# Another fixed order for layer 1, with sixteen more unread products, ten of them in a second bank, and ten instead of thirteen ahead of it

## The chip, the cores and the metric

One core of a Trainium2 chip runs the whole program. The core has five engines that each work through their own instructions in order: TensorE (PE, matmuls; its weight loads are listed as PEld), VectorE (DVE), ScalarE (ACT), GpSimd (POOL) and SyncE (SP), which here only starts DMA transfers. The metric is the device time of one execution in microseconds (us); lower is better.

## The reference

Three stages follow one another: an mLSTM, a gated layer and a normed gated layer.

```python
for t in range(S):                       # q, k, v: (2, 8, 768, 40)
    m_new = np.maximum(f_gate[:, :, t] + m, i_gate[:, :, t])
    f_stab = np.exp(f_gate[:, :, t] + m - m_new)
    i_stab = np.exp(i_gate[:, :, t] - m_new)
    C = f_stab[..., None, None] * C + i_stab[..., None, None] * np.einsum('bhd,bhe->bhde', vt, kt)
    n = f_stab[..., None] * n + i_stab[..., None] * kt
    y[:, :, t] = sigmoid(o_gate[:, :, t]) * (C @ qt) / np.maximum(np.abs(n . qt), 1.0)
x = y.transpose(0, 2, 1, 3).reshape(1536, 320)
x = (sigmoid(x @ w_gate) * (x @ w_val)) @ w_out            # layer 1: 320 -> 1536 -> 320
xn = x / np.sqrt(np.mean(x * x, -1, keepdims=True) + 1e-06) * rms_g
g = xn @ w_gate2
out = (g * sigmoid(g) * (xn @ w_val2)) @ w_out2            # layer 2: the same sizes
```

## The kernel before

The mLSTM is computed in six chunks c of 128 steps for each of the two batches b. A chunk needs scores (`S`, PE line 335), decays by a scan (`F`, DVE line 237), their product (`P`, DVE line 234), the part inside the chunk (`PV`, PE line 427), the part from the state (`I`, PE line 402) and a state update (`U`). Layers 1 and 2 run over twelve blocks f of 128 hidden columns. For layer 1, the operation `Tcf` (PE line 577, sixteen matmuls) multiplies chunk c by block f; for chunks 4 and 5 together it is `Tpf0` and `Tpf1` (PE line 623, eight matmuls of 512 columns each). `Y` operations multiply the hidden values by the block's output weights. Layer 2 starts inside the same fixed order with blocks 0 to 4 of its first four row tiles (`Tq`, `Yq`), and the rest of it is a loop over `seq` that is written behind the order.

Every input of a product is split into a rounded high part and a remainder. The hidden values get theirs from `H..1` (ACT, tile `fb`) and `H..2` (POOL, tile `ft`), after `S` (ACT), `M..1` and `M..2` (DVE). A weight block comes by one DMA (`LW` for layer 1, `LZ` for layer 2), is put together by `WT`/`ZT` (ACT or DVE) and `WM`/`ZM` (DVE), and then split by copies on ACT and subtractions on DVE and POOL. A layer 2 block lands in a tile with the tag `wraw`, of which there are two buffers; the second part of layer 2's input takes one of these from the first `RL` on:

```python
t.append(p2.tile([128, WC], I64, tag="wraw", name="wraw").bitcast(F32R)[:, 0:6 * T])
```

The program's order is a string, `PLAN`: a list of operation names, emitted from left to right. Each engine, and SP's queue of transfers, runs its own operations in exactly that order. Six names that are missing from it (`LATE`) are emitted in the loop's first pass. In that first pass (i = 5) the loop does the two products of block 5 and then the output product of block 4, whose hidden values come from `Hq41` and `Hq42`:

```python
        if i == NP:
            for m in range(2):
                w_up(k, f, m)
        ...
        for n in split[i - 1][0]:
            r_out(*seq[i - 1], n)
```

Some products are unread: `WARM` of them stand ahead of everything (line 975), and the operations `D0`, `D1`, ... (line 582) multiply the same constant tile into the bank of `T00`, which `T00` overwrites later. They change no result.

Of the kernel before, what the change touches and what calls it, by code (L numbers as in the profile page):

```python
# [51 lines left out]
Rgc XR00 WG2 Lqk10 WO0 WM0 WR0 Lfd D13 D14 D15 D16 D17 XP00 D18 LW4 D19 WLS2 WLS0 Lf11 WLR2 WLG2 WLR0 WT1 WG0 Lf10 D20 D21 WM1 WO1 Ltok10 WLH0 Lqg10
S10 XH00 XH01 WLG0 D22 D23 Lqg11 Lf12 WG1 XL00 XL01 T02 WT4 TS02 WLH1 UC01 WR1 T00 TS00 O10 LW3 Lf13 F11 F10 P10 I10 TH02 P11 IH10 Lqk11 Ltok11 WOH2
WLG1 LW5 V10 PV11 PV10 WLR1 TH00 WO4 WM4 UM01 H10a I11 IH11 WLS1 K11 K10 F12 F13 T01 Y000 Y021 Y001 WT3 WR4 TS01 S11 WO3 WM3 A10 WG4 WLG4 WG3 V11 WR3
Ltok20 LW6 TH01 P12 Y020 P13 H10r Y010 WLR3 H10b WLH3 WLG3 WLS3 PV12 PV13 Lqg20 Lqk20 LW8 Lf21 Lqk31 U10 H11a T03 WT5 O11 A11 H10c XR10 XP10 XH10 H11r
WLR4 WM5 WO5 WR5 WOH4 WLS4 WLH4 TS03 T04 Y011 H11b H11c XL10 TH03 WLS5 K12 K13 UC10 XR11 XP11 XH11 TS04 Y030 Y031 U11 XL11 T14 WT6 TH040 TH041 WG5 TS14
TH140 WM6 TH141 WOL4 WOL2 WO6 UC11 TH042 WOH6 T11 TS11 WG6 WR6 T12 Y041 WLG5 WLH5 TH142 WLH6 WLG6 WOH0 TH11 Y040 F21 WLR6 TS12 WT8 TH120 WLR5 WO8 UM10
LW7 Lf20 LW9 WT7 WM8 Y111 S20 P21 Y141 T10 WG8 TS10 TH10 Lf22 T15 Y110 WOH1 F20 Y140 LWb Ltok21 Lf33 LWa WT9 WOH5 WR8 WOH3 TH121 K21 WLS6 K20 TS15
TH150 TH151 WLR8 WM7 WO7 WLH8 V20 TH152 WLS8 T16 I20 Y100 T05 P20 PV20 Y101 TH122 WLG8 IH20 WR7 WG7 O21 TS05 TH050 WM9 WO9 TH051 TS16 TH052 TH160 F22
T06 PV21 TS06 O20 H20a A20 WG9 Y121 H20b V21 Y120 T08 H20r H20c TH060 WOL5 Y151 Y150 WOL6 WLG9 TH161 TH061 WR9 WOH7 T18 Y051 TH162 TH062 WLH7 WLS7 WLS9  # L60
TS18 Lqk21 Lf23 S21 Y050 TS08 Ltok30 Lqg21 F23 Y061 Y060 Y161 Lf31 WLR7 TH180 TH080 WLR9 WTb TH081 TH082 WOH8 TH181 WTa T19 WOL8 TH182 Y180 T13 Y160
WMa WOH9 TS19 TH190 P22 WOa K22 WLG7 UM11 F31 WOL3 Lqk30 WMb WOb WGa TH191 WOL7 TH192 TS13 TH130 P23 Y181 T07 Y081 I21 U20 IH21 T17 PV23 WRb WOHb WLRb
WGb XR20 TS07 WRa WOL9 Y190 PV22 Y191 TH070 WLGb TH071 WLGa WLSb WLSa WOHa K23 K31 TH072 Lf30 Lqg30 Y080 T1b H21a WLRa UC20 TS17 A21 TH131 TH132 TH170
H21r TS1b H21b H21c UM20 V30 T1a Y130 S30 TH171 V030 TH172 F30 TH1b0 P30 K30 V130 Y131 Y071 Y070 XP20 P030 TH1b1 TS1a TH1b2 TH1a0 WOLb XR21 XH20 T0b
TS0b TH1a1 P130 WOLa TH1a2 Y171 Y1b0 T0a XL20 P31 TH0b0 P031 Y1a1 XP21 Y170 U21 Y1a0 Lf32 F32 P131 F33 V230 P230 O30 TS0a TH0b1 XH21 TH0a0 P231 XL21
TH0b2 WOL0 Y1b1 T09 N110 N100 N101 P331 TS09 TH090 TH091 TH0a1 T23 T24 N102 V330 WOL1 TH0a2 UC21 N103 P330 I30 PV31 PV30 IH30 H30a TS23 A30 H30r Y0a0
Y0b1 H30b TH230 TH092 Y0a1 Ltok31 V31 V031 N111 LZ0 Lqk40 TS24 K33 UM21 N112 K32 Y090 Y0b0 N000 S31 Ltok41 Lqg31 H30c TH240 P33 P32 N001 U30 Y091 O31
Ltok40 TH231 N113 Lf41 XR30 P033 TH232 V131 UC30 N002 T27 TS27 TH270 N003 V231 TH241 Lf40 TH242 V331 N010 P032 P132 P133 TH271 N011 T25 T29 ZT0 TS25
T20 I31 F41 TH250 P233 TH272 P333 TS20 P232 P332 N012 N013 F40 K40 V41 Y270 T22 Y231 Y230 PV33 PV32 TH251 TH200 IH31 Y241 U31 T21 Y240 H31a H31b Lf43
A31 H31r UC31 XP30 TH252 Y250 Y271 V40 TS22 TH220 TH221 XH30 V040 H31c K41 Lqk41 Lf42 Lqg40 S40 TH222 XL30 TH201 UM30 TS21 TH202 V140 T28 Y221 U40 Y201  # L70
Y220 Y200 TH210 P40 P41 F42 P040 P041 XR31 P141 P241 V240 TS29 TH211 TH212 UC40 XP31 Y251 V340 P140 O40 XH31 P240 P341 XL31 T2a P340 TS2a TH2a0 F43
TH2a1 I40 Y210 PV40 PV41 Y211 T26 K42 TH2a2 TH290 TH291 TH292 IH40 H40a A40 H40b H40r H40c Lqk50 Ltok50 Lf50 Lqg41 V041 TS28 TH280 TH281 S41 Y2a1 Y291
Y290 UM40 TH282 V141 TS26 P42 TH260 P43 TH261 P042 P043 TH262 UM31 V241 V341 P143 T2b Y2a0 TS2b Lf51 TH2b0 P142 T30 TH2b1 P243 TS30 TH300 P343 P242
TH2b2 K43 Y280 T32 P342 F50 Y260 Y2b0 N200 N201 Y281 I41 TS32 TH320 PV43 PV42 Y261 TH301 O41 IH41 H41a V50 TH302 N202 Lqg50 F51 N203 Y2b1 T31 S50 I50
Lf52 Lqg51 Lqk51 Lf53 N210 Ltok51 V050 TS31 A41 TH321 N211 H41b P50 N212 TH322 V150 V250 V350 T36 T38 TH310 H41r P51 P051 IH50 P050 N213 H41c TS36 U41
P151 P150 XR41 TH311 P251 TH360 UC41 P250 Y301 T37 Y321 Y300 P350 P351 PV51 F52 PV50 XP41 H50a TH312 V51 T33 TH361 V051 TH362 V151 XR40 TS37 XH41 V251
Y360 Y361 S51 TS33 XL41 F53 TH330 TH370 TH371 Y311 XP40 Y310 P52 O50 O51 P53 ZM0 P053 P052 XH40 P152 XL40 P153 A50 H50r H50b V351 UM41 TH372 T39 Y370
TS39 P252 TH331 TH332 T3a Y320 TH390 TH391 P253 I51 IH51 P353 TS38 H50c XR50 T34 TH392 Y391 Y371 P352 TS3a TH3a0 TH380 LZ3 TH3a1 Y390 PV53 PV52 ZT3
TH381 T35 XP50 TH382 TH3a2 LZ4 H51a H51b A51 TS34 H51r H51c TH340 XH50 XL50 Y381 Y380 Y330 Y3a0 TS35 TH350 XR51 XP51 XH51 ZT4 TH341 ZM3 XL51 ZM4 TH342
T3b LZ2 Tp00 Sp0 ZT2 Tp01 Tp30 Y341 Tp31 Y331 Y3a1 Mp02 ZM2 LZ1 TS3b ZT1 Tp20 TH3b0 Y340 ZM1 LZb LZ5 Hp01 Sp3 TH3b1 TH3b2 Mp32 Hp31 Tp10 Tp11 Y3b1 Hp02  # L80
Y3b0 Hp32 Sp2 Sp1 ZTb Mp12 TH351 TH352 Y351 Y350 N300 N310 N301 N302 N311 Tp21 Yp33 N312 N303 Mp22 N313 Tp60 Yp30 Yp32 Yp31 Yp00 Yp03 Yp01 Yp02 ZG3 ZR3
Tp70 Tp61 Hp11 Hp21 ZT5 ZM5 ZLG3 Hp12 Hp22 Yp20 Yp13 Yp21 Yp22 Yp23 Yp11 LZ6 ZR0 ZO3 Sp7 ZO0 ZOL0 ZLS0 ZG0 ZT6 ZLS3 ZOL3 ZLR3 ZLG0 ZR2 Sp6 ZLR0 Mp62
Tp71 Yp12 Yp10 ZO2 Hp61 ZG2 ZM6 Mp72 Hp71 RR2 ZG1 ZO1 ZR1 ZLS2 Hp62 ZLH3 Tp40 Sp4 Yp62 Yp60 Tp41 Yp63 RP2 Yp61 Hp72 Tp50 Yp70 ZLS1 ZLH2 ZLG2 ZG6 LZ7
ZLG1 Mp42 ZOL1 ZT7 ZLG6 Tp51 Tpa0 Yp72 Yp71 RR0 Hp41 Hp42 Yp41 ZLH6 ZR6 Yp73 ZLR2 ZLR6 ZLR1 ZOL2 ZO6 RH2 ZOL6 ZM7 Sp5 Mp52 ZMb Tpa1 Yp40 Yp42 Yp43 Spa
ZR7 ZG7 ZLS7 Hp51 Hp52 Mpa2 Hpa1 ZO4 ZLH7 ZLS6 ZOL4 Tpb0 Yp51 RP0 LZ8 ZLR7 RL2 Yp53 Yp50 ZO7 RR3 RH0 ZT8 ZG4 Spb RL0 ZLG4 Tpb1 Mpb2 Yp52 Tp80 Tp90 ZR4
ZLR4 RP3 ZG5 ZLG5 ZR5 ZO5 ZLR5 Hpb1 RH3 RR1 Hpa2 ZLG7 ZLS4 ZOL5 ZLS5 ZOL7 RL3 Sp8 Hpb2 Ypa2 Tp81 RP1 Mp82 Ypb3 Ypb2 Ypb0 Ypa1 Ypb1 RH1 RL1 ZM8 Hp81 ZOb
Hp82 Ypa3 Tp91 Ypa0 Yp80 ZGb ZLGb Sp9 Mp92 Hp91 Hp92 ZLHb Tq20 Yp83 LZ9 Sq2 ZT9 ZM9 Mq21 Yp82 Yp81 ZO8 ZOL8 Yp91 N410 ZR8 Yp90 N400 ZG8 N401 N411 Yp92
# [1085 lines left out]
```

## Time and profile before

| | us |
|---|---|
| median of 3 runs | 468.8 (467.41 to 470.43) |
| the profiled execution's own time | 473.64 |
| its span, first to last instruction | 471.9 |
| PE busy in the span | 459.9 (97%) |
| DVE, ACT, POOL busy | 267.9, 202.2, 217.6 |

The profiled execution is a single one; its span leaves out 1.7 us of its own time. Its page has the busy share of each engine in 40 slices and the clock that PE was granted in each; the views used below are timelines of one engine, tables of short stretches, and who waited for whom. PE has two clock levels, 2.4 GHz (1.00 in the tables) and 1.2 GHz (0.50).

### The profile page before, as it was taken

The page shows a single profiled execution, that of the slowest core. Times are in us where ns is not written, and L with a number is a line of the kernel's source. Part 1 is how long each engine was busy: PE and PEld are TensorE (multiplying, and loading weights), DVE is VectorE, ACT ScalarE, POOL GpSimd, SP SyncE. Part 2 cuts the span into 40 slices and gives each one's busy share as a digit, 9 for nine tenths or more (in the row PEclk, how much of TensorE's full clock was granted, in tenths as well). Part 3 has the DMA queues.
Part 4 walks back from the last instruction along what each step waited for, and adds up shares of the span by engine and source line. Part 5 has one row for each costly group of instructions (what it writes and reads, how often), then busy time and mean ns, then how long its engine had stood idle before and what let it go on. Part 6 is the DMA issues. An engine that isn't in the chain of part 4 may idle for free.

```text
span 471.9 us, 9838 instructions
## 1 busy us (share of the span) xinstructions
PE 459.9 (97%) x3922; PEld 415.2 (88%) x3922; DVE 267.9 (57%) x464; ACT 202.2 (43%) x454; POOL 217.6 (46%) x269
## 2 busy tenths in 40 slices
...
PEclk9986999999999999999999999999999999999999
...
GB/s 237 300 302 330 285 162 188 70 39 66 95 185 96 104 39 111 85 225 193 85 83 85 0 163 6 1 33 35 1 57 3 18 35 18 49 9 1 1 2 58
DMA packets 19588, 45.50 MB, mean 96 GB/s; under 512 B 7926, under 2 KB 11398, under 8 KB 19542
## 3 DMA queue, kind: packets, MB, share of 16 engines
...
q8 instruction: 31, 0.51, 0.4%
...
q14 instruction: 15, 0.12, 0.1%
...
## 4 chain that ended last, share of the span: by engine, by line
PE 92%; DMA 4%; DVE 2%; ACT 1%; issue 1%; SPq 0%; POOL 0%; DVEq 0%; POOLq 0%
PE g L577 14%; PE o L645 12%; PE g L645 12%; PE a L645 10%; PE o L604 8%; PE g L623 7%; PE a L623 7%; PE o L729 6%; PE o L577 3%; PE a L427 2%; PE a L335 2%; DMA early<-in_qg_dram 2%; DMA fb<-fd 2%; PE o L601 2%; PE a L425 1%; PE o L975 1%
## 5 line engine op out<-in xcount | busy, mean ns | idle before, releaser
L134 POOL TENSOR_TENSOR ft<-p,fb 128x512 fp32r<-128x512 f32 x47 | 61.5, 1311 | 116.5 <-ACT fb L240 116.5
L577 PE MATMUL g<-xT,w 128*128 128x256 f32 x640 | 85.0, 288 | 1.5 <-ACT xT L240 0.8
L577 PEld LDWEIGHTS g<-xT,w 128*128 128x128 f32 x640 | 81.0, 195 | 2.5 <-ACT xT L240 1.3
L234 DVE TENSOR_TENSOR p<-p,g 128x512 f32<-128x512 f32 (+1 forms) x37 | 24.9, 673 | 96.6 <-ACT p L702 94.5
L645 PE MATMUL a<-xT,w 64*128 64x512 f32 (+1 forms) x310 | 79.1, 382 | 0.0
L645 PE MATMUL g<-xT,w 64*128 64x512 f32 (+1 forms) x310 | 79.0, 382 | 0.0
L702 ACT ACTIVATE p<-g 128x512 f32<-128x512 f32 x47 | 28.1, 597 | 79.1 <-PE g L645 61.6
L134 POOL TENSOR_TENSOR h<-sig,h 128x256 fp32r<-128x256 f32 x42 | 36.7, 877 | 50.8 <-ACT h L240 48.6
L645 PE MATMUL o<-w,fb 64*128 64x320 f32 (+1 forms) x508 | 57.7, 307 | 0.0
L240 ACT ACTIVATE fb<-p 128x512 fp32r<-128x512 f32 (+1 forms) x49 | 30.3, 622 | 63.7 <-DVE p L234 53.6
L645 PEld LDWEIGHTS g<-xT,w 64*128 64x128 f32 x310 | 53.9, 184 | 3.8
L645 PEld LDWEIGHTS a<-xT,w 64*128 64x128 f32 x310 | 53.8, 184 | 3.7
L645 PEld LDWEIGHTS o<-w,fb 64*128 64x128 f32 (+1 forms) x508 | 45.2, 185 | 5.4 <-issue 0.5
L604 PE MATMUL o<-w,h 128*128 128x320 f32 x252 | 47.0, 318 | 0.0
L234 DVE TENSOR_TENSOR p<-p,a 128x512 f32<-128x512 f32 (+1 forms) x49 | 33.1, 676 | 20.5 <-PE a L623 12.8
L645 PE MATMUL a<-wraw,w 64*128 64x512 f32 (+1 forms) x155 | 44.5, 383 | 0.0
L645 PE MATMUL g<-wraw,w 64*128 64x512 f32 (+1 forms) x155 | 44.5, 383 | 0.0
L645 PE MATMUL o<-w,ft 64*128 64x320 f32 (+1 forms) x254 | 39.3, 304 | 0.0
L604 PEld LDWEIGHTS o<-w,h 128*128 128x128 f32 x252 | 37.8, 189 | 1.1
L134 POOL TENSOR_TENSOR w<-wc,w 128x256 fp32r<-128x256 f32 (+2 forms) x37 | 26.1, 714 | 23.1 <-ACT w L240 15.9
L645 PEld LDWEIGHTS g<-wraw,w 64*128 64x128 f32 x155 | 28.2, 185 | 3.7
L645 PEld LDWEIGHTS a<-wraw,w 64*128 64x128 f32 x155 | 28.2, 185 | 2.5
(176 smaller groups left out, 907.5 us busy)
## 6 DMA issues: line engine op xcount, KB each, us to landing
...
```

Of the source, the lines that this page charges most:

```text
L134: eng.tensor_tensor(out=out, in0=a, in1=b, op=ALU.subtract)
L234: eng.tensor_tensor(out=out, in0=a, in1=b, op=op)
L240: a_.activation(out=out, in_=x, func=AF.Copy, scale=scale)
L335: nc.tensor.matmul(out=st[j][:, i * L:(i + 1) * L], lhsT=t[n, 1, i, :], rhs=t[n, 0, i, :], start=True, stop=True)
L427: nc.tensor.matmul(out=ps[:, (o + i) * E:(o + i + 1) * E], lhsT=p[:, i, :], rhs=w[:, o + i, :], start=True, stop=True)
L577: nc.tensor.matmul(out=g[:, m, :], lhsT=w[:, m, ws, :], rhs=x[xs // 3][:, xs % 3, :], start=(i == 0), stop=(i == 7))
L601: nc.tensor.matmul(out=o, lhsT=h[:, b * L:(b + 1) * L], rhs=o32[f], start=(n == 1), stop=(n == NF))
L604: nc.tensor.matmul(out=o, lhsT=h[:, hs, b * L:(b + 1) * L], rhs=wo_t[f][:, ws, :], start=(n == 1 and i == 0), stop=(n == NF and i == 2))
L623: nc.tensor.matmul(out=g, lhsT=w[:, m, ws, :], rhs=x[xs // 3][:, xs % 3, :], start=(i == 0), stop=(i == 7))
L645: k = nc.tensor.matmul(**kw).ins
L702: a_.activation(out=s, in_=keep["w", k, f, 0], func=AF.Sigmoid)
L729: nc.tensor.matmul(out=o_ps[key][:, 0:DM], lhsT=h[hs][:, n], rhs=wo_t[f][:, ws, :], start=(c == 1 and i == 0), stop=(c == NF and i == 2))
```

## The change

`PLAN` is another order of the same operations, with six more `D` and ten new ones, `E0` to `E9`, which multiply the constant tile into bank `o2` instead. The products ahead of the order are ten instead of thirteen. `LATE` holds three names instead of six; the other places of `PLAN` change everywhere.

```diff
-WARM = 13
+WARM = 10
...
-ND = 24
+ND = 30
+NE = 10
...
 PLAN = """
...
-N512 Tq30 Tq10 Sq1 Tq31 Tq11 Yq21 Yq02 Yq00 ZOLa ZLS8 ZLH9 Mq11 N513 ZGa ZLRa Mq12 Yq03 Yq20 Yq23 Yq22 Yq01 Tq40 Tq41 ZLS9 ZLR9 Sq3 Mq31 Mq32 Hq31 Hq32
-Yq31 Yq32 Yq33 ZLGa Hq11 Hq12 Yq13 Yq30 Sq4 Mq41 Yq12 Yq11 Mq42 ZLG9 Hq41 Hq42 Yq10
...
+Yq11 Yq33 Yq12 ZTa ZMa ZOa ZLG5 ZRa Sq4 ZGa ZLGa Mq41 ZLS7 Yq13 ZOb ZLSa ZLH6 LZ8 ZLRa ZOLb ZLR7 ZT8 ZM8 ZG8 ZLG8 ZR8 ZLR8 Mq42 ZOLa Yq32 Yq30 Hq41
+Hq42
 """
...
-LATE = "ZOLb ZLR8 ZOL9 ZRb ZLRb ZLSb"
+LATE = "ZLS8 ZO8 ZOL8"
...
+    def m_idle2():
+
+        if "idle" not in keep:
+            keep["idle"] = bank("o2")
+        nc.tensor.matmul(out=keep["idle"], lhsT=warm[:, 0:128], rhs=warm, start=True, stop=True)
...
     for k in range(ND):
         op(f"D{k}", m_idle)
+    for k in range(NE):
+        op(f"E{k}", m_idle2)
```

**First place: SP's queue near the start.** The names are the destination tile and the source; `wraw` from `in_w_dram` is a weight block of layer 1 (blocks 0, 1 and 4 before; 2, 0, 1 and 3 after), `fd` a store of the decays, which the loads into `fb` and `early` from `fd` read back, and `early` from `in_qg_dram` the queries that `I10` (PE line 402) reads. Before:

```order
L247 DMA gates<-in_gate_if_dram 80x256
L247 DMA rmsg<-in_rms_g_dram 128x320
L184 DMA wraw<-in_w_dram 128x3839
L269 DMA gates<-in_cst_dram 80x150
L184 DMA wraw<-in_w_dram 128x3839
L141 DMA raw<-in_qk_dram 40x1024 x2
L247 DMA fd<-gates 80x128
L184 DMA wraw<-in_w_dram 128x3839
L174 DMA fb<-fd 128x512
L174 DMA early<-fd 128x512
L155 DMA early<-in_tok_dram 128x976
L163 DMA early<-in_qg_dram 120x384
```

After, in the same part of SP's queue:

```order
L264 DMA gates<-fm 80x129
L186 DMA wraw<-in_w_dram 128x3839
L271 DMA gates<-in_cst_dram 80x150
L186 DMA wraw<-in_w_dram 128x3839
L249 DMA fd<-gates 80x128
L186 DMA wraw<-in_w_dram 128x3839
L143 DMA raw<-in_qk_dram 40x1024 x2
L176 DMA early<-fd 128x512
L176 DMA fb<-fd 128x512
L157 DMA early<-in_tok_dram 128x976
L186 DMA wraw<-in_w_dram 128x3839
L165 DMA early<-in_qg_dram 120x384
```

The store to `fd` now stands ahead of a weight block and the next scores' inputs, the load of `rmsg` (0.16 MB) has gone to a later place, and the first weight block stands behind `gates<-fm` instead of ahead of it.

**Second place: PE, from the last unread product to the fourth layer 1 product.** The first row is two products `T02` and `T00`, L402 is an `I`, L427 (L429 after) a `PV`, the last row `T01`. Before:

```order
L582 MATMUL g<-gates 128x512
L577 MATMUL g<-xT,w 128x256 x32
L402 MATMUL a<-cm,early 128x126 x2
L402 MATMUL a<-cm,early 128x84
L427 MATMUL a<-vv,p 128x42 x8
L402 MATMUL a<-cm,early 128x126 x2
L402 MATMUL a<-cm,early 128x84
L577 MATMUL g<-xT,w 128x256 x16
```

After:

```order
L584 MATMUL g<-gates 128x512
L579 MATMUL g<-xT,w 128x256 x32
L429 MATMUL a<-vv,p 128x42 x8
L404 MATMUL a<-cm,early 128x126 x2
L404 MATMUL a<-cm,early 128x84
L579 MATMUL g<-xT,w 128x256 x16
```

Both `PV` now stand ahead of `I10`, and `I11` stands behind `T01`.

**Third place: ACT at the end of the fixed order.** An `fb` is the high part of hidden values (`fb_3720` is `Hq31`, `fb_3799` is `Hq41` of the changed kernel; `fb_3778` is `Hq41` before), `top` from `wraw` is a `ZT`, a `w` from `raw` or `wc` the high part of a weight block, and `p` from `g` an `S`. Before, up to the loop's first `S`:

```order
L240 ACTIVATE w_3630<-raw_3628 128x2x256
L702 ACTIVATE p_3739<-g_3645 128x512
L240 ACTIVATE fb_3743<-p_3739 128x512
L240 ACTIVATE fb_3757<-p_3663 128x512
L702 ACTIVATE p_3767<-g_3719 128x512
L240 ACTIVATE fb_3778<-p_3767 128x512
L702 ACTIVATE p_3803<-g_3785 128x512
```

After:

```order
L242 ACTIVATE fb_3720<-p_3635 128x512
L198 ACTIVATE top1_83<-wraw_3702 128x960
L242 ACTIVATE w_3760<-raw_3758 128x320
L242 ACTIVATE w_3760<-raw_3758 64x128 x2
L710 ACTIVATE p_3765<-g_3732 128x512
L242 ACTIVATE w_3760<-raw_3758 128x2x256
L242 ACTIVATE w_3479<-wc_3006 128x320
L198 ACTIVATE top0_82<-wraw_3777 128x960
L242 ACTIVATE w_3785<-wc_3783 128x2x256
L242 ACTIVATE w_3785<-wc_3783 64x128 x2
L242 ACTIVATE fb_3799<-p_3765 128x512
L710 ACTIVATE p_3821<-g_3803 128x512
```

The two `ZT` of blocks a and 8 now stand between `Hq31` and `Hq41`; before, both were done well ahead of this place.

## Rows read from the trace of the kernel before

**Rows 1.** The page: TensorE's busy time, and its granted clock in 40 equal slices (tenths).

```profile
PE 459.9 (97%) x3922; PEld 415.2 (88%) x3922; DVE 267.9 (57%) x464; ACT 202.2 (43%) x454; POOL 217.6 (46%) x269
...
PEclk9986999999999999999999999999999999999999
```

**Rows 2.** Busy time by stretch of 1 us, then granted clock (PEclk), DMA share, GB/s.

```profile
32.00:33.00 1.00, 0.33 (x2) 0.36 (x3) 1.00 (x3) 0.56 (x2) 1.00 (x2) 0.85 1.02 327
...
42.00:43.00 1.00, 1.00 (x4) 0.80 (x4) 0.91 (x3) 0.51 (x3) 0.00 (x0) 0.53 1.06 379
43.00:44.00 1.00, 1.00 (x5) 0.58 (x4) 0.31 (x1) 1.00 (x3) 0.31 (x1) 1.00 0.99 347
```

**Rows 3.** Timeline of PE, 20 to 48 us: start, us, instruction [idle before, releaser].

```profile
20.22 1.24 PE L582 MATMUL g<-gates 128*128 128x512 bf16 x5
...
26.85 3.50 PE L577 MATMUL g<-xT,w 128*128 128x256 f32 x27 [0.70 <-DVE xT L134]
32.67 1.52 PE L402 MATMUL a<-cm,early 120*128 120x126 f32 x6 [2.32 <-DMA early<-in_qg_dram]
33.99 3.55 PE L427 MATMUL a<-vv,p 128*128 128x42 f32 x16
...
38.61 3.76 PE L577 MATMUL g<-xT,w 128*128 128x256 f32 x16
42.17 2.16 PE L601 MATMUL o<-o,h 128*128 128x320 f32 x6
...
46.54 1.88 PE L427 MATMUL a<-vv,p 128*128 128x42 f32 x16
```

**Rows 4.** Timeline of SP's transfer issues, 20 to 24 us.

```profile
20.01 0.32 SPq L247 DMA_DIRECT2D fd<-gates  x1
20.37 0.43 SPq L184 DMA_DIRECT2D wraw<-in_w_dram  x1
...
23.30 0.90 SPq L163 DMA_DIRECT2D early<-in_qg_dram  x2
```

**Rows 5.** Timeline of DVE, 25 to 40 us.

```profile
25.79 1.01 DVE L134 TENSOR_TENSOR xT<-o,xT 128x384 fp32r<-128x384 f32 x2
...
32.38 0.68 DVE L234 TENSOR_TENSOR p<-a,ft 128x512 f32<-128x512 f32 x1
...
39.35 1.22 DVE L237 TENSOR_TENSOR_SCAN ft<-early,ident 128x512 f32<-128x512 f32 x1
```

**Rows 6.** Timeline of PE, 97 us.

```profile
97.44 0.81 PE L433 MATMUL a<-vv,kk 128*120 128x126 f32 x6 [1.44 <-DVE p L234]
```

**Rows 7.** Timeline of all engines, 270 to 306 us.

```profile
270.73 1.15 DVE L203 SCALAR_TENSOR_TENSOR wc<-wraw,top 128x960 int32<-128x960 int32 x1
...
271.94 7.68 SPq L184 DMA_DIRECT2D wraw<-in_w_dram  x2
...
276.65 1.03 DVE L198 CAST top<-wraw 128x960 f16<-128x960 bf16 x1 [1.65 <-DMA wraw<-in_w_dram]
...
284.20 1.30 ACT L196 ACTIVATE top<-wraw 128x960 f16<-128x960 bf16 x1
...
290.57 0.63 ACT L240 ACTIVATE w<-raw 128x512 fp32r<-128x512 f32 x1
...
294.58 0.69 DVE L234 TENSOR_TENSOR p<-p,a 128x512 f32<-128x512 f32 x1
...
295.19 0.68 DVE L134 TENSOR_TENSOR w<-raw,w 128x512 fp32r<-128x512 f32 x1
...
302.78 1.29 POOL L134 TENSOR_TENSOR ft<-p,fb 128x512 fp32r<-128x512 f32 x1 [3.06 <-ACT fb L240]
302.84 0.45 PE L729 MATMUL o<-w,fb 128*128 128x320 f32 x2
303.28 1.31 PE L623 MATMUL g<-xT,w 128*128 128x512 f32 x5
305.12 1.30 PE L623 MATMUL a<-xT,w 128*128 128x512 f32 x5
```

More of the change, by code (lines that the diff above doesn't have):

```diff
@@ L44 @@
 NP = 5
-ND = 24
+ND = 30
+NE = 10
 PLAN = """
-Lga Gm Gf1 Gf2 Gfe Gmz Gfh D0 D1 D2 D3 Lgs Gms Gid Ltok00 Gse Gi1 Gfl Gie O00 Gt Fb00 D4 D5 Fb03 Gtg Lqk00 Lqk01 Ltok01 Rm Lms LW2 Lmr Lgr Lrms LW0 F00
-Fb02 D6 Fb01 F02 S01 S00 F01 F03 P01 K00 V00 K02 K01 P03 O01 D7 D8 U00 D9 UC00 K03 V01 UM00 PV01 PV03 A03 A01 Lsel P02 P00 H01a H03a H01r WT2 Ri1 H01b
-H03r H03b Rie LW1 WM2 D10 PV00 Rf1 Rf2 PV02 A02 Rfe D11 D12 U01 H00a H02a H02r H02b Rer Rt1 Rc1 WO2 XR01 A00 H00r H00b WT0 Rel Rz Rt2 XP01 Rg Rc2 WR2
@@ L52 @@
[L52 to L87, printed above, removed]
@@ L88 @@
-Tq21 Tq00 ZLG8 Mq22 Hq21 LZa Sq0 Yp93 Tq01 N402 N412 Hq22 N413 Mq01 Mq02 N403 N500 ZTa ZR9 Hq01 ZMa ZRa ZG9 ZO9 N510 ZOa N501 N502 N503 N511 Hq02 ZLSa
-N512 Tq30 Tq10 Sq1 Tq31 Tq11 Yq21 Yq02 Yq00 ZOLa ZLS8 ZLH9 Mq11 N513 ZGa ZLRa Mq12 Yq03 Yq20 Yq23 Yq22 Yq01 Tq40 Tq41 ZLS9 ZLR9 Sq3 Mq31 Mq32 Hq31 Hq32
-Yq31 Yq32 Yq33 ZLGa Hq11 Hq12 Yq13 Yq30 Sq4 Mq41 Yq12 Yq11 Mq42 ZLG9 Hq41 Hq42 Yq10
+Lgr Lga Gm Gi1 Gie Gid D0 D1 D2 D3 D4 D5 D6 D7 D8 Lgs Gse Gf1 Gms Gf2 Gfe Gmz Gfh Rm Gfl Fb02 F02 Lqk00 Ltok01 D9 D10 D11 Gt Gtg Fb00 Lqk01 O01 Lms S00
@@ new lines @@
+F00 P00 V01 Ltok00 Lmr S01 P02 O00 Fb01 LW2 D12 D13 Fb03 D14 F01 P01 F03 PV02 D15 D16 D17 D18 D19 Ri1 Rie V00 K02 Rf1 Rf2 K00 Rfe H02a Rer PV01 K01 A02
+A01 WT2 H01a H02r H02b K03 U00 Lsel LW0 Rz Rel H01r H01b Rt2 Rc2 UC00 U01 Rt1 PV00 E0 E1 E2 E3 D20 D21 UM00 XR00 Lfd Rc1 WM2 P03 WO2 PV03 H00a LW1
+Lqk10 Lf10 Lf11 Ltok10 A00 H00r H00b XP00 WT0 WM0 WO0 WR2 WG2 LW3 Lqg10 A03 XH00 WLS2 WLR2 H03a H03r H03b WR0 WG0 D22 WLH0 WLS0 E4 E5 E6 D23 E7 E8 WLR0
+WLG2 XL00 LW4 Lf12 Lqk11 WLG0 Lf13 XR01 Rg D24 E9 D25 D26 D27 XP01 D28 WT1 Rgc XH01 WM1 XL01 S10 WO1 WR1 D29 O10 T02 TS02 WOH2 F11 F10 P10 WLR1 P11 V10
@@ new lines @@
+K11 WLS1 Ltok11 WG1 WLG1 WLH1 TH02 T00 WT3 TS00 UC01 WT4 PV10 PV11 I10 TH00 WM3 IH10 H10a T01 WO3 UM01 Lqg11 WO4 WM4 TS01 WR3 A10 WG3 O11 WG4 WOH4 WR4
+TH01 K10 LW6 F12 WLS3 V11 WLH3 WLG3 Y000 Y020 Y001 Y011 S11 F13 P12 P13 LW5 Lqk20 Ltok20 WLH4 WLS4 Y010 Y021 I11 H10r WLR3 WLG4 PV13 K13 IH11 H10b PV12
+H10c XR10 WLR4 H11a A11 H11r H11b H11c T03 WOL4 K12 XP10 U10 UC10 UM10 T04 WT6 TS03 TH03 XR11 XP11 XH10 XL10 TS04 TH040 XH11 Y031 Y030 U11 XL11 TH041
+TH042 T11 WT5 Lf21 LW8 T10 Y041 Y040 WO5 WM5 WR5 TS11 WM6 WO6 TH11 WR6 WLR5 WLR6 UC11 WG6 WOH5 WOH3 WG5 TS10 T14 Lf20 Y110 S20 TS14 F20 TH140 LWa
@@ new lines @@
+Ltok21 LW9 Y111 T12 WOL2 V20 Lqg20 WLG5 WLS5 WLH5 WLG6 WLH6 F21 P21 TH10 P20 TH141 TS12 TH120 WT8 T15 T05 WT9 TH121 K20 WLS6 TH142 TH122 WO8 TS15 WM8
+TS05 TH050 TH150 I20 Y101 Y100 T16 Y120 Y140 Y121 T06 PV20 Y141 Lf30 LWb Lf22 Lqk21 LW7 Lqg21 WO9 WM9 WOH6 WR8 WG8 TH051 WOH8 TH151 WOL5 UM11 K21 WLH8
+TH052 V21 WG9 TH152 WR9 TS06 TH060 WLS8 WLG8 O21 TH061 TS16 WLR8 WOL8 TH160 O20 F22 WLR9 WOL6 WLG9 Y050 WT7 WTa TH062 T18 PV21 Y051 T08 Y150 Y151 WLS9
+TH161 TH162 Y061 Y160 Y161 Lf23 TS18 TH180 WO7 IH20 WM7 WOa H20a TS08 TH181 T19 K22 S21 TH182 WR7 WG7 WLS7 WLG7 TS19 WLR7 F23 TH080 TH190 P23 WMa P22
@@ new lines @@
+T13 U20 Y181 Y060 WLH7 T07 WTb WOH7 TH081 TH082 WMb TS13 WRa TH191 WOHa TH192 UC20 WOb TH130 WGb WLGb WGa WLGa F30 Y080 Y180 Y081 T17 I21 TS07 TH070
+K23 TH131 TH132 WRb TH071 TH072 WLSa PV23 PV22 H20b WLRb WLRa T1a A20 H20r IH21 H21a Lqk30 Lf31 LZ0 Lqk50 Ltok30 Lrms Lf32 F31 Lqg30 Lf40 WOH9 TS17
+WOHb A21 WOLb H20c TH170 WOL7 WLSb Y071 S30 Y070 T1b TS1a WOH0 XR20 H21r P31 P031 TH171 WOL3 WOLa Y130 P30 P030 TH1a0 WOL9 Y131 Y190 K31 TH172 V30 XP20
+TS1b P130 TH1b0 TH1b1 Y191 TH1a1 TH1a2 TH1b2 K30 H21b F32 P131 H21c WOH1 P231 XR21 P230 T0b T09 XH20 V030 V130 TS09 Y1a0 Y170 P330 UM20 XL20 TH090 Y1b0
@@ new lines @@
+TS0b XP21 XH21 N100 TH0b0 XL21 N101 Y1b1 Y171 Y1a1 T0a U21 V230 O30 TH091 TH0b1 N110 F40 Lf33 Lqk31 V330 TH092 TS0a TH0a0 TH0a1 T23 PV30 T24 N102 TH0a2
+UC21 TS23 TH0b2 Y0a1 TH230 N111 P331 N103 TS24 TH240 Y0b1 Y0b0 I30 PV31 Y090 Ltok31 V31 N112 WOL0 UM21 Y091 Ltok40 WOL1 K32 O31 IH30 H30a H30b N113 U30
+S31 T27 Y0a0 Lqg31 A30 N010 H30r N011 P32 F33 P33 TH231 ZT0 TH241 P032 TH232 T25 V031 P033 N012 TH242 V131 K33 TS27 TS25 N000 UC30 P132 N013 TH250
+TH270 P232 P332 N001 T20 TH251 V231 P133 P233 P333 TH252 N002 V331 T29 T22 I31 N003 IH31 Ltok41 V40 Y241 Y240 Y251 Y230 PV32 Lf41 Lqk40 Lqg40 TS20 F41
@@ new lines @@
+PV33 Y250 TH271 TH200 TH272 H30c H31a Y271 Y270 U31 S40 TH201 XR30 TS22 TH220 TH221 V040 Lf42 UM30 TH202 TH222 K40 UC31 T28 T2a Y231 XP30 P40 P41 H31b
+P040 TS29 P041 TS28 TH290 P141 K41 V41 V140 F42 T21 A31 TH291 P241 V240 XH30 TH292 V340 XL30 TS21 TH210 H31r P140 TH280 Y221 Y220 U40 P341 UC40 T26
+TH211 TH212 K42 UM40 Y290 Y211 I40 H31c PV41 P240 IH40 Y201 Y200 TS26 XR31 TH260 P340 XP31 Y291 TH281 TH261 TH262 TH282 UM31 PV40 H40a T2b Y260 O40
+XH31 Lf43 Lf51 Lqk41 S41 V041 TS2a Y210 Y280 Y261 Y281 XL31 TH2a0 F51 TS2b T30 P42 TH2b0 TH2b1 V141 V241 P042 TH2b2 Y2b1 T32 Y2b0 V341 F43 K43 P43 P142
```

16 lines of the change are left out of this document (added).

## The prediction

> **What bounds the kernel now.** I read the page first, then PE's waits, then stretches of 1 us where PE is idle or its clock is low. The page says that PE is busy for 459.9 of 471.9 us [rows 1]: PE's own queue sets the time, and what another engine does counts only where PE waits for it. A new order of the same products can therefore win only PE's idle time and its time at the low clock, and can lose only by new waits.
>
> PE's idle time lies in few places. In the first 33 us it waits for short spells, the longest being the 2.32 us ahead of `I10` at 32.67, which waited for a transfer [rows 3]. Behind that there is one wait over a microsecond up to the last loop: 1.44 us at 97.44, for DVE [rows 6].
>
> The low clock is one stretch. In the second from 32 to 33 the mean is 0.85, in that from 42 to 43 it is 0.53, and at 43 it is 1.00 again; the slices between show the drop [rows 1, 2]. So PE runs at 1.2 GHz from about 32.8 to 42.5, with two `I`, two `PV`, `T01` and the start of the first `Y` behind one another without a gap [rows 3]. A stretch of 9.7 us in which PE always works costs half of itself at half the clock: **4.8 us**. (The two `PV` bear this out: 33.99 to 37.5 there, 1.88 for the next two at 46.54.)
>
> The profiled execution took 473.64 us. Less 4.8 it would be 468.8, which is the median of the runs shown. I take it that the runs without a profile mostly don't have this stretch. The sum is made for both: against 473.64 the stretch goes as a term of its own, against 468.8 it is zero.
>
> **Part 1: up to the first layer 1 products.** Thirteen more unread products come ahead of `T02` (three fewer warm ones, sixteen more). Five of them take 1.24 [rows 3], at most 0.25 each, so at most 3.2 us of PE. They stand where PE waits: `T02` starts its second half at 26.85 because the remainders of its input come from DVE, 25.79 to 26.80 [rows 3, 5], and that hangs on ACT and DVE work that the new order hardly shortens. The last of PE's waits there is the 0.70 ahead of this second half. Cost of the products: nothing while that cover holds, and 3.2 us at most without it. For the release of `T02` I walked the queues of the first 27 us with the durations of the trace. On the one side the first weight block now waits for `gates<-fm` and comes 2 to 3 us later in SP's queue, and the ten `E` wait for ACT to empty bank `o2`; on the other the store to `fd` is issued earlier. It comes out between 0.5 us earlier and 1 us later; I take no change.
>
> **Part 2: from `T02` to `T01`.** Before, the store to `fd` was issued at 20.01, a weight block behind it at 20.37 and the queries of `I10` last at 23.30 [rows 4], which is why `I10` waited until 32.67. The new queue has the store ahead of a weight block, and one load of 0.16 MB less, so the transfers have no hole at 20 us; I estimate the queries 3 to 4 us earlier, and both `PV` stand ahead of `I10` too. The DMA wait goes. What is late next is DVE: after the remainders (26.80) it does a small copy, two scans and a product before the first `PV`, 0.5 + 2 x 1.22 + 0.68 = 3.6 [rows 5], so 30.4, and a second product with a small subtraction before the other, 31.5. The second `PV` (half of 1.88) ends at 32.4, `I10` (half of 1.32, its time at the low clock from 32.67 to 33.99) at 33.1, `T01` (half of 3.76) at 35.0 [rows 3]. `I11` now comes later, and with its 0.7 the comparable time is 35.7. Before, at the full clock, `T01` would have ended 4.7 before its 42.17 (half of the time since 32.8), at 37.5. **The gain is 1.8 us, and 2.3 if `T02` comes 0.5 earlier; I take 2.0, between 1 and 3.3.** In the profiled execution the 4.8 us come on top, as no idle spell as long as 2.32 us is left here.
>
> **Part 3: the middle, 45 to 270 us.** Every engine's order changes, and I found no transfer or buffer that must come late. The wait of 1.44 us [rows 6] may go, or one like it may come, as DVE has to do the same work in less time. I take zero, from -1.4 (the wait gone) to +2.
>
> **Part 4: the end of the fixed order.** Of the two `wraw` buffers one holds layer 2's input by then, so the blocks load one at a time: at 270.73 a block is put together for 1.15 us, and the next load is issued at 271.94 and has landed at 276.65, 4.71 us [rows 7]. The new order puts blocks a and 8 last, and on ACT both `ZT` stand between `Hq31` and `Hq41`. That is a chain in which each step must wait for the one before. `Hq31` needs an `fb` buffer that the last `Yq2` product frees; call its end zero. Then `Hq31` 0.63, `ZTa` 1.30, `ZMa` 1.15, load of block 8 4.71, `ZT8` 1.30, `ZM8` 1.15, `ZG8` 0.63, `ZLG8` 0.68, `Mq42` 0.69, `Hq41` 0.63 [rows 7]: 12.9 us. With a small subtraction (`ZLR8`, a quarter of the size of `ZLG8`, some 0.3) and nine handoffs of 0.05 (0.06 lie between the end of the block's work and the load), 13.6. `Sq4` and `ZM8` stand in the same queues, so no engine can pass.
>
> From the same zero PE does `Tq41`, `Tq40`, eight `Yq` and the loop's two products of block 5: 4 x 1.84 (303.28 to 305.12) + 8 x 0.44 (302.84 to 303.28) = 10.9 us [rows 7]. Then it needs `Hq41`: **a wait of 2.7 us.** Two products later (0.3) it needs `Hq42` as well, 1.29 after `Hq41` on POOL: 1.0 more. Together **3.7 us**; from 3.0 (no handoffs) to 4.5 (a load that takes 5.5). The old order had both blocks done before. Just ahead of this `Tq11` waits for bank `a` until `Mq32`: behind `Tq21` DVE has three products of 0.69 and two small steps against PE's 0.44 + 1.84, so 0.3 more.
>
> **Sum.** Against the median: 468.8 - 2.0 + 0 + 3.7 + 0.3 = **470.8 us**. Against the profiled execution: 473.64 - 4.8 - 2.0 + 0 + 3.7 + 0.3 = 470.8.
>
> **Rivals.**
>
> *Slower: the clock falls at the new wait.* In the trace it fell after an idle spell of 2.32 us behind one of 0.70 [rows 2, 3], and did not after 1.44 [rows 6]. The new wait is 2.7 us, a short burst and 1.0: past the first. From the spell that fell, PE ran at half until 42.5, 4.8 us lost; if that comes again, 470.8 + 4.8 = 475.6. For a shorter fall speaks that the `T` from 38.61 was followed by the rise after 3.9 us, and the loop is dense at once: 1.9 lost, 472.7. [...]
>
> The Trainium skill ("TensorE: Matmul & The Clock Gate", section "HAM oscillation — how this bites in real kernels") speaks against the change here: waits of PE on transfers put its clock back to half, and the products behind them pay. By that rule the fall comes, and the time is one of these two, 472.7 or 475.6; the trace agrees with the fall at 32.8.
>
> *Faster: the end is hidden.* Were block 8 loaded or converted earlier than I read, or had PE other work, parts 1 and 2 remain: 468.8 - 2.0 = 466.8, and 465.4 with the middle's wait gone. Against it: `Hq41` stands behind `ZT8` in ACT's own queue.
>
> *The runs shown have the low clock too,* and a profile simply takes longer. Then the stretch's 4.8 us go as well: 466.0. Against it stands that 473.64 less 4.8 is the median.
>
> *The change doesn't do what it says:* the unread products leave the clock as low as in the trace, or the start comes late by their 3.2 us: 474.0 to 475.6.
>
> **How the numbers follow.** About 1% (4.7 us) is what a measurement of this kernel can tell from no change. The wait at the end without a long fall of the clock: 0.5 (470.8, of these a third at 472.7). A long fall: 0.15 (475.6). The end hidden: 0.18 (465.4 to 466.8). The low clock in all runs: 0.12 (466.0). The start failing: 0.05. Slower than 473.5: the long fall, the start, and a little of the forecast with a bad middle, 0.23. Faster than 464.1: the hidden end or the low clock with a good middle, 0.17. The rest, 0.6, is the same. The range goes from 464.7, a little below the hidden end, to 475.6, the long fall.
>
> **What the profile after would show.** Right: the clock at 1.00 from 25 to 50 us, no wait of `I10` on a transfer, `T01` done by 36; then one wait of PE on ACT's `fb` of 2 to 3 us and one on POOL's `ft` of about 1 just ahead of the loop, with a `top` on ACT that waited for `wraw`. Wrong: no such wait, PE waits over 2 us between 45 and 270, or a low clock at the start.

## The result and the profile after

The changed kernel took **472.9 us** (median of 8 runs, 470.39 to 473.79) against 469.75 for the kernel before (8 runs on the same chip): a ratio of 1.0072, 95% interval 1.0044 to 1.0100. It is 0.7% slower: clear of the noise by the interval, and less than the 1% that the prediction took as no change. 470.8 was forecast, between 464.7 and 475.6. The profiled execution took 473.75 us, with a span of 471.9.

Three lines of the page after answer to [rows 1]: PE's busy time, its busy share in 40 slices, and its clock.

```profile
PE 459.7 (97%) x3932; PEld 419.7 (89%) x3935; DVE 267.1 (57%) x464; ACT 203.0 (43%) x454; POOL 225.9 (48%) x269
...
PE   8999999999999999999999999699999999999996
...
PEclk9999999999999999999999999979999999999999
```

The low clock of the first slices is gone. A new place stands in the 26th slice (295 to 307 us): PE is idle for a third of it, and the clock falls to 0.7 in the next. PE's waits by what ended them (us in total, times, longest) name it:

```profile
PE o L653 <- ACT fb L242: 3.1, 1, 3.1
...
PE o L653 <- POOL ft L136: 0.8, 1, 0.8
```

**The end of the fixed order**, which answers to [rows 7]. First PE there in the timeline:

```profile
300.32 0.84 PE L631 MATMUL a<-wraw,w 128*128 128x512 f32 x3
304.22 0.56 PE L653 MATMUL o<-w,fb 64*128 64x320 f32 x4 [3.06 <-ACT fb L242]
305.57 0.64 PE L653 MATMUL o<-w,ft 64*128 64x320 f32 x2 [0.79 <-POOL ft L136]
...
306.80 0.63 PE L653 MATMUL g<-xT,w 64*128 64x512 f32 x1
```

Then ACT, on which the two `top` are `ZTa` and `ZT8` and the last `fb` is `Hq41`:

```profile
290.81 1.30 ACT L198 ACTIVATE top<-wraw 128x960 f16<-128x960 bf16 x1
...
298.53 1.30 ACT L198 ACTIVATE top<-wraw 128x960 f16<-128x960 bf16 x1 [2.58 <-DMA wraw<-in_w_dram]
301.06 1.16 ACT L242 ACTIVATE w<-wc 128x512 fp32r<-128x512 f32 x3 [1.22 <-DVE wc L205]
303.54 0.63 ACT L242 ACTIVATE fb<-p 128x512 fp32r<-128x512 f32 x1 [1.32 <-DVE p L236]
```

And SP's issue of block 8's load:

```profile
293.33 0.33 SPq L186 DMA_DIRECT2D wraw<-in_w_dram  x1
```

Block 8 is asked for at 293.33 and is there at 298.53 (5.2 us); `ZT8` waits for it, DVE waits for `ZT8`, ACT for DVE, and `Hq41` stands behind all that. PE stands still for 3.06 and then for 0.79.

The clock falls behind the first wait, at the second. By stretch of 1 us (busy time of PE, PEld, DVE, ACT, POOL; then the clock):

```profile
303.00:304.00 1.00, 0.00 (x0) 0.00 (x0) 0.45 (x1) 0.46 (x1) 0.00 (x0) 1.00 0.00 0
304.00:305.00 1.00, 0.56 (x4) 0.30 (x4) 0.31 (x1) 0.66 (x2) 0.75 (x1) 0.97 0.00 0
305.00:306.00 1.00, 0.43 (x2) 0.43 (x4) 0.90 (x2) 0.00 (x0) 1.00 (x2) 0.50 0.00 0
...
311.00:312.00 1.00, 1.00 (x10) 1.00 (x10) 0.00 (x0) 0.00 (x0) 0.00 (x0) 0.61 0.00 0
312.00:313.00 1.00, 1.00 (x12) 0.79 (x10) 0.00 (x0) 0.00 (x0) 0.00 (x0) 1.00 0.00 0
```

PE works at 1.2 GHz from 305.57 to about 311.8, and half of that is lost: 3.1 us. The end costs 3.85 + 3.1 = 7.0 us in all.

**The start**, which answers to [rows 3]:

```profile
26.30 1.16 PE L337 MATMUL a<-raw 40*128 40x128 f32 x14 [0.26 <-ACT gb L242]
27.43 4.17 PE L579 MATMUL g<-xT,w 128*128 128x256 f32 x32
32.05 2.04 PE L429 MATMUL a<-vv,p 128*128 128x42 f32 x16 [0.45 <-DVE p L236]
33.91 0.88 PE L404 MATMUL a<-cm,early 120*128 120x126 f32 x6
34.59 2.16 PE L579 MATMUL g<-xT,w 128*128 128x256 f32 x16
...
44.78 2.16 PE L579 MATMUL g<-xT,w 128*128 128x256 f32 x16
```

The wait of `I10` on its queries is gone. `T02` starts at 27.43, and `T01` is over at 36.6. Between 50 and 300 us the only wait left is one of 0.24 at 101.16, in place of the 1.44 of [rows 6].

**The runs of before fall into two groups by their mean granted clock.** Of 35 runs of before, 14 have 0.999 or more and lie at 466.69 to 468.73 (median 467.6); 21 have 0.984 to 0.993 and lie at 469.86 to 473.89 (median 470.3). So the median of before, 469.9, holds some 2.3 us of low clock, and a run at the full clock takes 467.6. Of the changed kernel every run is low, 0.989 to 0.996; the profiled one, 0.993, is low at the end alone, and of the others the mean does not say where they are low. The medians below mix such runs, so differences of under 1 us between them are not read.

### The profile page after: what moved, and what is told of

Its sections match the earlier page's. It is cut to its first block, busy times and chain, and to the rows that moved or that the text cites. A ratio compares the mean times of both kernels' runs of the same rounds, so it can differ in the third digit from the quotient of the medians.

```text
span 471.9 us, 9839 instructions
## 1 busy us (share of the span) xinstructions
PE 459.7 (97%) x3932; PEld 419.7 (89%) x3935; DVE 267.1 (57%) x464; ACT 203.0 (43%) x454; POOL 225.9 (48%) x269
## 4 chain that ended last, share of the span: by engine, by line
PE 86%; DMA 6%; DVE 3%; issue 2%; POOL 1%; ACT 1%; SPq 0%; POOLq 0%; DVEq 0%
PE g L579 15%; PE o L653 12%; PE a L653 11%; PE g L653 11%; PE o L612 8%; PE a L631 6%; PE g L631 6%; PE o L737 5%; DMA wraw<-in_w_dram 4%; PE o L579 3%; PE a L337 2%; PE a L427 1%; PE a L429 1%; PE o L404 1%; PE o L609 1%
## 5 line engine op out<-in xcount | busy, mean ns | idle before, releaser
L579 PE MATMUL g<-xT,w 128*128 128x256 f32 x640 | 83.9, 286 | 0.2 <-DVE r L458 0.2
L579 PEld LDWEIGHTS g<-xT,w 128*128 128x128 f32 x640 | 79.4, 191 | 1.1 <-ACT rem L242 0.5
L136 POOL TENSOR_TENSOR h<-sig,h 128x256 fp32r<-128x256 f32 x42 | 35.3, 843 | 61.6 <-ACT h L242 53.9
L653 PE MATMUL o<-w,fb 64*128 64x320 f32 (+1 forms) x508 | 58.8, 309 | 3.1 <-ACT fb L242 3.1
L653 PEld LDWEIGHTS g<-xT,w 64*128 64x128 f32 x310 | 55.2, 188 | 2.9
L653 PEld LDWEIGHTS a<-xT,w 64*128 64x128 f32 x310 | 55.2, 188 | 2.7
L653 PEld LDWEIGHTS o<-w,fb 64*128 64x128 f32 (+1 forms) x508 | 48.1, 188 | 6.8 <-ACT fb L242 3.5
L612 PE MATMUL o<-w,h 128*128 128x320 f32 x252 | 44.4, 315 | 0.0
L653 PE MATMUL o<-w,ft 64*128 64x320 f32 (+1 forms) x254 | 42.1, 314 | 0.8 <-POOL ft L136 0.8
L612 PEld LDWEIGHTS o<-w,h 128*128 128x128 f32 x252 | 37.5, 189 | 0.3
L136 POOL TENSOR_TENSOR w<-wc,w 128x256 fp32r<-128x256 f32 (+2 forms) x37 | 27.9, 761 | 12.0 <-ACT w L242 8.6
```

The costliest lines, as they stand in the source:

```text
L136: eng.tensor_tensor(out=out, in0=a, in1=b, op=ALU.subtract)
L579: nc.tensor.matmul(out=g[:, m, :], lhsT=w[:, m, ws, :], rhs=x[xs // 3][:, xs % 3, :], start=(i == 0), stop=(i == 7))
L612: nc.tensor.matmul(out=o, lhsT=h[:, hs, b * L:(b + 1) * L], rhs=wo_t[f][:, ws, :], start=(n == 1 and i == 0), stop=(n == NF and i == 2))
L653: k = nc.tensor.matmul(**kw).ins
```

## Experiments

### Block 8's conversion taken out of the way

```diff
-... ZLR7 ZT8 ZM8 ZG8 ZLG8 ZR8 ZLR8 Mq42 ZOLa Yq32 Yq30 Hq41
+... ZLR7 Mq42 ZOLa Yq32 Yq30 Hq41
-LATE = "ZLS8 ZO8 ZOL8"
+LATE = "ZT8 ZM8 ZG8 ZR8 ZLG8 ZLR8 ZLS8 ZO8 ZOL8"
```

> The changed kernel (472.9) with block 8's conversion (six operations) moved behind the loop's first pass, so that Hq41 and Mq42 no longer stand behind it on ACT and DVE. If the 0.7% come from the wait and the low clock behind it: 3.85 of idle time and some 2.9 of half clock go, 466.2. If the wait alone is lost and the low clock is not in the runs without a profile: 469.1. If the loss lies at the start or in the middle: 472.9, and the profile has no wait here either.

Measured: **465.7** (464.4 to 466.88, 12 runs), 0.9923 of before (0.9899 to 0.9948), 7.2 us less than the changed kernel. Both waits are gone, PE works without a gap, and the clock stands:

```profile
300.00:302.00 2.00, 2.00 (x20) 1.58 (x20) 1.03 (x2) 0.48 (x1) 1.34 (x3) 1.00 0.02 4
302.00:304.00 2.00, 2.00 (x24) 1.80 (x22) 0.61 (x1) 1.35 (x2) 1.30 (x1) 1.00 0.00 0
304.00:306.00 2.00, 2.00 (x24) 1.81 (x22) 1.27 (x3) 1.37 (x4) 0.12 (x1) 1.00 0.00 1
```

Nothing but the place of six operations off PE differs. So the end costs about 7, as the trace says, and without it the new order is 0.8% faster than the old one. A part of this is the low clock in the median of before: the six runs of this version at 0.999 or more have a median of 464.7, 2.9 (0.6%) under the 467.6 of before at the same clock. It is the best version of this study.

### The wait filled with unread products

```diff
             for m in range(2):
                 w_up(k, f, m)
+            keep["fill"] = bank("g")
+            for j in range(13):
+                nc.tensor.matmul(out=keep["fill"], lhsT=wg_t[f][:, 0, 0, :], rhs=xT[k][0][:, 0, :], start=True, stop=True)
```

The loop's next product takes over the same bank.

> The changed kernel with thirteen unread products of 512 columns, 0.22 each, put where PE waits for Hq41 (behind the loop's two products of block 5). Hq41 comes no earlier, so the idle time stays as time, but PE works in it. If the low clock behind the wait costs: 472.9 less 2.9, 470.0, and the clock stays at 1.00 from 300 to 320 us. If only the wait counts: 472.9. The wait of 0.8 for ft stays in both.

Measured: **470.2** (467.76 to 474.09, 12 runs), 1.0027 of before (0.9997 to 1.0057), 2.7 less than the changed kernel. PE in the timeline:

```profile
304.54 3.11 PE L1052 MATMUL g<-xT,w 128*128 128x512 f32 x13
307.58 0.56 PE L653 MATMUL o<-w,fb 64*128 64x320 f32 x4
308.77 0.42 PE L653 MATMUL o<-w,ft 64*128 64x320 f32 x2 [0.63 <-POOL ft L136]
```

The thirteen products take about the time of the wait (3.11 for 3.06), the 0.63 for `ft` is still there, and the clock is 1.00 in each stretch from 300 to 320 us. So the cost of the end splits into the wait, 3.85, and the clock, about 3; this version takes 4.5 more than the one with block 8 late, near the wait's 3.85. (This one execution took 474.09, since its clock fell at the start; the last section comes back to it.)

### Six instead of thirteen

> The changed kernel with six unread products instead of thirteen in PE's wait for Hq41: 1.35 us of it are filled, some 1.7 stay idle. If the clock falls only behind a spell of about 2 us: it stands, and the time is that with thirteen, 470.2. If shorter spells do as well: it falls, 472.9.

Measured: **469.7** (468.13 to 472.02, 12 runs), 1.0003 of before (0.9977 to 1.0030). The wait is cut in two:

```profile
300.72 1.52 PE L1052 MATMUL g<-xT,w 128*128 128x512 f32 x6
303.43 0.56 PE L653 MATMUL o<-w,fb 64*128 64x320 f32 x4 [1.19 <-ACT fb L242]
304.78 0.41 PE L653 MATMUL o<-w,ft 64*128 64x320 f32 x2 [0.79 <-POOL ft L136]
```

and the clock stays, by stretch of 2 us:

```profile
302.00:304.00 2.00, 0.80 (x6) 0.30 (x4) 0.76 (x2) 1.12 (x2) 0.54 (x1) 1.00 0.00 0
304.00:306.00 2.00, 1.22 (x14) 1.13 (x16) 1.27 (x2) 0.59 (x2) 1.62 (x3) 1.00 0.00 0
306.00:308.00 2.00, 2.00 (x24) 1.75 (x22) 1.32 (x1) 0.41 (x2) 1.80 (x2) 1.00 0.00 0
```

1.19 and 0.79, with 0.56 of work between them, did not let it fall; 3.06 and 0.79 did. The execution's mean clock of 0.996 comes from the start (0.73 from 35 to 40 us).

### Without the sixteen further unread products

The operations `E0` to `E9` and `D24` to `D29` go out of the order, nothing else.

> The changed kernel without its sixteen further unread products (E0 to E9, D24 to D29). If they lie in PE's waits and the clock stands without them: 472.9, within 0.5. If they keep the clock up at the start: up to 4.8 more, 477.7. If they push T02 back: 16 x 0.22 less, 469.4.

Measured: **472.2** (471.58 to 472.73, 12 runs), 1.0055 of before (1.0031 to 1.0078): no difference from the changed kernel that can be told. The trace shows two effects that nearly cancel. On the one side a `PV` of the start comes at 18.97 instead of 20.50 (19.64 in the trace with block 8 late). On the other PE now waits 1.96 for DVE before 23.71, and from then on the clock is down (0.84 in the mean from 20 to 25 us, 0.50 from 25 to 30):

```profile
23.71 0.47 PE L500 MATMUL o<-cs,x 128*128 128x128 f32 x1 [1.96 <-DVE x L462]
...
27.41 5.31 PE L579 MATMUL g<-xT,w 128*128 128x256 f32 x32
...
43.82 2.16 PE L579 MATMUL g<-xT,w 128*128 128x256 f32 x16
```

`T02` starts at 27.41, as with the sixteen (27.43), but behind scores that take 2.88 at the low clock, so this does not show that the sixteen cost nothing by themselves. `T02` then takes 5.31 instead of 4.17, but the `PV` behind it waited for DVE anyway, and the product at 44.78 comes at 43.82. The low clock costs little here, where PE is not the one who is late. At the end the waits of 2.74 and 0.71 and the fall behind them (0.50 from 304 to 310) are there again.

Both edits together, without the sixteen and with block 8 late:

> The changed kernel with block 8's conversion behind the loop's first pass (465.7) and without the sixteen further unread products. If these change nothing, as 472.2 against 472.9 says: 465.0 to 465.7. If they hold the clock in stretches in which PE sets the time: 468 or more.

Measured: **466.5** (465.74 to 467.56, 12 runs), 0.9934 of before (0.9908 to 0.9961), against 0.9923 with the sixteen. Its runs all have a mean clock of 0.987 to 0.993, those with the sixteen 0.995 or more. In both traces without the sixteen the clock is 0.50 from 25 to 30 us, and in none of the four with them, so the sixteen do hold it there. Their net worth is less than the runs can tell: 0.7 less without them at 472.2, 0.8 more without them at 466.5.

### The queries of `I10` loaded earlier, in the kernel before

```diff
-... XP00 D18 LW4 D19 ... Ltok10 WLH0 Lqg10
+... XP00 D18 Lqg10 LW4 D19 ... Ltok10 WLH0
```

> The kernel before with the queries of I10 loaded ahead of a weight block, nothing else moved. If the runs without a profile have the low clock from 32.8 on as the profile of before has it: 469.75 less 4.8 and about 1.5 of the wait (DVE is late next), 463.5. If they don't have it: 468.0 with DVE next, or 467.4 with the whole wait gone. If the load hidden before now delays the weight block that T01 needs: 469.75 or more. The profile shows PE's wait of 2.32 on the queries gone or not.

Measured: **469.9** (467.33 to 472.73, 12 runs), 1.0016 of before (0.9987 to 1.0044): nothing. Again four runs are at 467.3 to 467.9 with the full clock, and eight at 469.9 and above with 0.987 to 0.993. So the fall of the clock does not hang on when that transfer is issued. The profiled execution is one of the four. In it `I10` waits 0.69, for DVE, and the first scan on DVE 0.55 for the decays; whether the wait on the queries comes back in a run with a low clock is not shown. The queries were not the only late transfer in the profile of before, either. DVE waited there too, for the decays:

```profile
29.00 1.23 DVE L237 TENSOR_TENSOR_SCAN ft<-fb,ident 128x512 f32<-128x512 f32 x1 [2.20 <-DMA fb<-fd]
```

### The kernel before, profiled a second time

> The kernel before once more, unchanged, for a second profiled execution of it. If the wait of 2.32 on the queries and the low clock behind it belong to the order: both come again, span near 471.9. If they belong to that one execution: the wait is under 1.5 and the clock stands or falls without it, span 466 to 469.

Measured: 467.9 in one run, span 466.0, the clock at 1.00 throughout. PE in its timeline:

```profile
26.85 3.48 PE L577 MATMUL g<-xT,w 128*128 128x256 f32 x27 [0.70 <-DVE xT L134]
30.95 0.90 PE L402 MATMUL a<-cm,early 120*128 120x126 f32 x6 [0.62 <-DVE p L234]
31.97 1.95 PE L427 MATMUL a<-vv,p 128*128 128x42 f32 x16
...
34.42 2.16 PE L577 MATMUL g<-xT,w 128*128 128x256 f32 x16
36.42 1.78 PE L601 MATMUL o<-o,h 128*128 128x320 f32 x6
...
42.88 2.17 PE L577 MATMUL g<-xT,w 128*128 128x256 f32 x16
...
91.50 0.81 PE L433 MATMUL a<-vv,kk 128*120 128x126 f32 x6 [1.46 <-DVE p L234]
...
301.14 0.56 PE L645 MATMUL o<-w,fb 64*128 64x320 f32 x4
...
302.12 0.39 PE L645 MATMUL g<-xT,w 64*128 64x512 f32 x1
```

The 2.32 of [rows 3] is not there: `I10` waits 0.62, for DVE, and `T01` is over at 36.4. The wait on the queries does not come in every execution; in how many it does is open. The wait of 1.46 before 91.50 is the same as that of [rows 6], so this one belongs to the order. In this execution DVE does not wait for the decays, and its two scans ahead of `I10` take 1.77 and 1.69.

### The kernel before with the end of the changed one

```diff
-... N500 ZTa ZR9 Hq01 ZMa ... Hq31 Hq32 Yq31 Yq32 Yq33 ZLGa Hq11 Hq12 Yq13 Yq30 Sq4 Mq41 Yq12 Yq11 Mq42 ZLG9 Hq41 Hq42 Yq10
+... N500 ZR9 Hq01 ... Hq31 Hq32 Yq31 Yq32 Yq33 Hq11 Hq12 ZTa ZMa ZOa ZRa Yq13 Yq30 Sq4 ZGa ZLGa Mq41 LZ8 ZLSa ZLRa ZOLa
+ZT8 ZM8 ZG8 ZLG8 ZR8 Yq12 Yq11 Mq42 ZLG9 Hq41 Hq42 Yq10
```

`ZO8`, `ZOL8` and `ZLS8` go to `LATE`.

> The kernel before with the end of the changed one: blocks a and 8 of layer 2 last, block 8's load behind block a's conversion and its own conversion ahead of Mq42 and Hq41 on DVE and ACT. If that chain is the cost, in whatever order: 469.9 + 3.85 + 2.9 = 476.6, with a wait of PE on fb of 3 to 5 and half clock behind it. If it needs the rest of the new order to cost anything: 469.9 to 471.

Measured: **473.7** (473.14 to 477.03, 4 runs), 1.0104 of before (1.0054 to 1.0154).

```profile
307.65 0.56 PE L645 MATMUL o<-w,fb 64*128 64x320 f32 x4 [2.92 <-ACT fb L240]
309.00 0.42 PE L645 MATMUL o<-w,ft 64*128 64x320 f32 x2 [0.79 <-POOL ft L134]
```

The same two waits come up in the old order, 3.71 together, and the clock falls behind them, here for a shorter time (0.91 from 308 to 310, 0.50 from 310 to 312, 0.74 from 312 to 314). Against the runs of before at the full clock, 467.6, that is 6.1 more; against the median, 3.8. The expected 476.6 was counted from the median, which holds low clock already; from 467.6 the same sum gives 474.4.

## Why the prediction was right, and where it was off

The two executions that can be compared term by term are the changed kernel (span 471.9) and the second profile of before (466.0), 5.9 apart. Each term stands on one execution of each kernel.

| step | forecast | shown |
|---|---|---|
| Part 1, unread products | 0 | 0 (net, from the medians, within 0.8) |
| Part 2, start | -2.0 | +2.1 |
| Part 3, middle | 0 (-1.4 to 2) | -2.1 |
| Part 4, waits on `Hq41`, `Hq42` | +3.7 | +3.85 |
| Part 4, wait of `Tq11` | +0.3 | 0 |
| the clock at the end | 0 (rival: 1.9 or 4.8) | +3.1 |
| the loop | not counted | -1.1 (with block 8 late) |
| sum | +2.0 | +5.9 |

**Part 4 held.** The chain of `Hq31`, both `ZT`, the load and `Hq41` is in the trace, step by step; its waits measured 3.06 and 0.79 for a forecast of 2.7 and 1.0. The load took 5.2 and not 4.71, and most of the difference is that. Taking the chain away gave back 7.2; putting it into the old order brought the waits up there. `Tq11` never waited.

**The rival on the clock came, with a size between its two.** It was given a third of the chances, and it should have been the forecast: the trace of before had a fall behind 2.32, and the new wait was forecast at 2.7, with a second one behind it. The Trainium skill ("TensorE: Matmul & The Clock Gate", section "HAM oscillation — how this bites in real kernels") tells of waits of PE on transfers that put its clock back; the waits in its example are longer than the one forecast, so it did not settle the question. The trace agrees that the clock falls behind such a wait: 0.97 in the stretch from 304, 0.50 from 305. PE stayed low for some 6 us, and 3.1 were lost; filling the wait gave back 2.7 to 3.2.

**Part 2 failed, and so did the step of the bound that fed it.** It took the low clock out of the start of before, but kept the wait of 2.32 as what the order does. That start came from one profiled execution, at 473.64 slower than all but one of the 35 runs. The second profile has `T01` over at 36.4 and not at the 37.5 that was worked out for the full clock. The change then took 1.6 longer than forecast: `T01` ends at 36.6, not 35.0 (and not by the 36 that was named as a sign of being right). What was left out is, above all, what stands ahead of the first `PV` on DVE: the two scans start at 28.25 behind two steps of a weight block, and the second takes 1.72, not 1.22:

```profile
28.25 1.21 DVE L239 TENSOR_TENSOR_SCAN ft<-fb,ident 128x512 f32<-128x512 f32 x1
29.39 1.72 DVE L239 TENSOR_TENSOR_SCAN ft<-early,ident 128x512 f32<-128x512 f32 x1
31.21 0.69 DVE L236 TENSOR_TENSOR p<-a,ft 128x512 f32<-128x512 f32 x1
```

The prediction had the first `p` done at 30.4; it is done at 31.9. On PE `S10` waits for ACT to empty bank `a` (`gb`) until 26.30, and `T02` starts 0.6 later than the second half did before. Not all of that is the order's: in the trace with block 8 late, with the same order there, `T02` starts at 26.81, the first `PV` at 31.42, and it has waited for DVE as well (0.44). Up to the product at 44.78 (42.88 in the second profile; 0.6 of an update comes later there, and two `Y`, 0.4, come earlier) the new order is 2.1 behind: 0.9 by the end of `T01`, with `I11` counted in, and 1.2 behind it, where PE waits 0.43 and 0.37 for DVE. That these two queues are the whole cause was read from the trace and not tried by moving them.

**Part 3 went to its good end and past it.** The new order has the 2.1 back by 301.16, where the second profile stands at 301.14. The wait of 1.46 at 91.50 and one of 0.40 at 133.20 are gone, and one of 0.24 is new, which makes 1.6 of it; the rest is not assigned.

**The low clock of before.** The prediction took it as missing from the runs without a profile. It is in 21 of 35, at a price of 2.7 and not 4.8, so the rival that the runs have it too held in part. That 473.64 less 4.8 gave the median was chance: the two profiles of before are 5.75 apart at the end of `T01` (42.17 and 36.42), 1.7 of it by the wait and the rest, 4.0, behind it, where the clock was low; and the three runs that gave 468.8 were too few, as 35 give 469.9. The low clock in the runs is why the medians lie only 3.0 apart. It is also how 470.8 came within 2.1 of the result: the terms were off by 3.9 in all (start +4.1, clock +3.1, `Hq41` and `Hq42` +0.15, middle -2.1, loop -1.1, `Tq11` -0.3), and the base at the full clock is 467.6 and not 468.8, which makes 470.8 + 3.9 - 1.2 = 473.5 for the 472.9 measured. The size of the new wait was right, and by its mechanism, and the direction with it. That the total came so near was luck: large errors of both signs stood behind it.
